# Gathers of the next expert moved, in pairs, to the first products of the present one, in a pooled-attention and mixture-of-experts kernel

## The chip, the cores and the metric

One NeuronCore of a Trainium2 chip runs the whole program. The metric is the device time of one execution in microseconds (us), inputs and output in HBM. TensorE (PE) multiplies, VectorE (DVE) and ScalarE (ACT) work on tiles in SBUF and PSUM, GpSimd (POOL) does some sums and issues the indirect transfers (gathers and scatters by a list of rows), and SyncE (SP) issues the plain transfers. Each engine takes its instructions strictly in order and waits for others by semaphores. SP's and POOL's transfers share 16 DMA engines.

## The reference

```python
# attention with keys and values pooled over 8 tokens, then:
logits = x @ w_gate
noisy = logits + log1p(exp(x @ w_noise)) * noise
top2 = the two best experts of each token; top2_w = softmax of their two values
out = 0
for e in range(8):
    for k in range(2):
        mask = top2[:, k] == e
        h = maximum(x[mask] @ w1[e], 0)              # 512 -> 1024
        out[mask] += top2_w[mask, k, None] * (h @ w2[e])   # 1024 -> 512
```

There are 4608 tokens of 512 numbers, so an expert sees about 1152 of them. Everything is float32.

## The kernel before

**Order of the work.** Attention comes first, then expert 0, then experts 1 to 7 one after another. Products are made of three TensorE passes on operands split into a high and a low part (ACT casts the high part, DVE subtracts to get the low part; function `parts`, lines 1336 and 1337).

**An expert is a list of 44 items.** `first_products(e)` makes items g0 to g0+21: the first layer of seven 128-token tiles, done with seven block products in place of eight (their sums are made by `sums_a` on POOL, from the quarters of w1, and by `sums_b` on DVE, from the quarters of the turned rows). The products come in the order A12·B21 (g0, g0+1), A11·B11 (g0+2, g0+3), four tail products (g0+4 to g0+7, the first layer of tiles 7 to 9), S1·T1 (g0+8, g0+9), S2·T2, S4·B22, S3·T3, four tail products, A22·T4 (g0+20, g0+21). From m0 = g0+22 on come the second-layer items: two for each of seven tiles (`second_tile`, m0 to m0+13), then eight of the second tail (`second_tail`, line 1502, m0+14 to m0+21). In expert 7 the second tail comes ahead of the tiles. A tail's width is chosen at run time from the expert's count of rows: 240 columns in experts 1, 6 and 7, 280 in 3 and 5, 304 in 2 and 4.

**Operand buffers.** Every item reads one or two of eight buffers `OPS`. `build(i)` fills, in order of use, every buffer that item i has set free, as soon as `ripe` and `gate` allow. So DVE and ACT work up to eight operands ahead of TensorE. The main loop writes, for each item: its matmuls, then what `todo` holds for it (`on(i, f)`), then its `after` (results read out of PSUM), then `build(i)`.

**The next expert's rows.** Each tile of 128 rows takes a chain: a POOL gather from x_dram into one of two `row` buffers (line 771), four SP writes into one of four `via` buffers in HBM (776), one SP load into one of four `xg` buffers (779), and then DVE's block transpose (`turn_rows`, 1308; for tiles 7 to 9 `tail_rows`, lines 818 to 823, with an ACT cast and a DVE subtraction). Before the change tiles 0 to 3 are gathered at g0+15 and g0+18, tiles 4 to 9 one by one at m0+1 to m0+8, each in the same place in which an earlier tile is turned; tails are turned at m0+10 to m0+12.

**Second-layer results.** `prev` (line 1124) gathers with POOL what a token's first visit left in slot_dram, into one of three `pv` buffers; `finish` adds the new result on DVE (1140) and lets POOL write it to slot_dram (1144) and scatter it to the output (1148). Before, `prev` for tile n+3 stands behind `finish` of tile n, and takes the same buffer.

**What sets the order.** PE, DVE, ACT and POOL run this part in the order in which the code stands (`manual_schedule`). SP's order is a scheduler's, with `turn_of` chaining some transfers. SP also loads w1 (`load_w1`, 1298) and halves of w2 (`wload`, 470), which ACT and DVE split at lines 490 and 491, one step every other item from g0+1 to g0+15.

Of the kernel before, what the change touches and what calls it, by code (L numbers as in the profile page):

```python
# [19 lines left out]
def kernel(  # L20
# [12 lines left out]
    nc = tc.nc  # L33
# [4 lines left out]
    P = 128  # L38
# [709 lines left out]
    XG = {}  # L748
    turns = {}

    def turn_of(q, make):
        if q in turns:
            with tc.issue_after(turns[q].ins):
                turns[q] = make()
        else:
            turns[q] = make()
        return turns[q]
# [25 lines left out]
    NM = 7  # L783
# [555 lines left out]
    def side_a(e, name, k):  # L1339
        def make(t):  # L1340
            src = sx(k) if name in ("S1", "S2") else {"A11": W1R[:, 0, k], "A12": W1R[:, 0, 2 + k], "A21": W1R[:, 1, k], "A22": W1R[:, 1, 2 + k],
                   "S3": W1R[:, 0, k], "S4": W1R[:, 0, 2 + k]}[name]
            parts(src, DF // 2, t)
            if name == "A11":
                sums_a(k, 1)
            elif name == "S1":
                sums_a(k, 2)
        return make

    def side_b(e, name, k):  # L1350
        def make(t):
            src = {"B11": XR1[:, 0, k], "B21": XR1[:, 0, 2 + k], "B22": XR1[:, 1, 2 + k], "T1": XR1[:, 0, k],
                   "T2": XR1[:, 0, k], "T3": XR1[:, 1, k], "T4": XR1[:, 0, 2 + k]}[name]
            parts(src, HN, t)
            if name == "B11":
                sums_b(k, 1)
            elif name == "T1":
                sums_b(k, 2)
        return make

# [108 lines left out]
    def second_tile(e, tt, n):  # L1469
        for j in range(2):  # L1470
            key = (e, "h", tt, j)
            makers[key] = side_h(tt, j)

            def run(j=j, key=key):
                if j == 0:
                    st[e, "y"] = bank()
                py = st[e, "y"]
                for f in range(4):
                    for i, (a, b) in enumerate(PASSES):
                        mm(py, at[key][:, a * DF // 2 + f * P:a * DF // 2 + (f + 1) * P], w2s(e, b, 4 * j + f),  # L1480
                           j == 0 and f == 0 and i == 0, j == 1 and f == 3 and i == 2)

            def after():
                finish(e, tt, P, st[e, "y"], st[e, "pv"].pop(0))
                if n + 3 < NM:
                    st[e, "pv"].append(prev(e, TILES[n + 3], P))
            item([key], run, after if j else None)

    def second_tail(e):
# [40 lines left out]
    def on(i, f):  # L1530
        todo.setdefault(i, []).append(f)

    def flush():
        with tc.issue_after(sent[-1].ins):
            nc.gpsimd.drain()

    gate, ripe = {}, {}
    for e in range(1, E):
# [21 lines left out]
        for i in range(8):  # L1560
            on(g0 + 1 + 2 * i, lambda: wadvance(1))
        for i in range(4 if e == 1 else 3):
            on(g0 + 8 + 2 * i, lambda: pend.pop(0)())
        if final:
            for i in range(3):
                on(m0 + 5 + 2 * i, lambda: pend.pop(0)())
# [2 lines left out]
            st[e, "pv"] = [prev(e, TILES[n], P) for n in range(3)]  # L1569
        on(m0 - 2, start_pv)  # L1570
        if e == 1:
            def visits2():
                with tc.issue_after(st["dve"].ins):
                    second_visits()

            def over2():
                with tc.issue_after(st["dve"].ins):
                    st["over"] = over_table()
            on(g0 + 9, visits2)
            on(g0 + 16, over2)  # L1580
        if not final:
            n = e + 1
            on(g0 + 15, lambda n=n: gathers(n, 0, 1))
            on(g0 + 18, lambda n=n: gathers(n, 2, 3))
            for i, j in ((0, 1), (0, 0), (1, 0), (1, 1)):
                on(m0, lambda n=n, i=i, j=j: load_w1(n, i, j))
            plan_ = ((1, 0, 4), (2, 1, 5), (4, 2, 6), (5, 3, 7), (7, 4, 8), (8, 5, 9), (9, 6, None))
            for d, a, b in plan_:
                on(m0 + d, lambda n=n, a=a: turn_rows(n, a))
                if b is not None:  # L1590
                    on(m0 + d, lambda n=n, b=b: gathers(n, b))
            for i in range(3):
                on(m0 + 10 + i, lambda n=n: tail_rows(n))
            on(m0 + 13, lambda: (sums_a(0, 0), sums_a(1, 0)))
            gate[n] = m0 + 13

    for i, g in enumerate(groups):
        if joined(g):
# [12 lines left out]
            gathers(1, 4, 5, 6)  # L1611
        elif i == 0:
            stage2(g, lambda t, mm: hook(i, t, mm), None)
    for i in range(3):
        on(i, lambda: tail_rows(1))
    on(2, lambda: (sums_a(0, 0), sums_a(1, 0)))
    gate[1] = -1
    ripe[1, "S1"] = 2

    def ready(key, i):  # L1620
        e = key[0]
# [25 lines left out]
            makers[key](OPS[s])  # L1647

    ET = mybir.EngineType
    with tc.manual_schedule(engines={ET.PE, ET.DVE, ET.Activation, ET.Pool}):  # L1650
        for t in range(4, NM):
            turn_rows(1, t)
        gathers(1, 7, 8, 9)
        build(-1, ())
        stage2(groups[2], None, None)
        TB.append(mp.tile([P, NFB * DF], F32, tag="hb", name="tb"))
        for i, (keys, run, after) in enumerate(items):
            build(i - 1, keys)
            run()
            for f in todo.get(i, ()):  # L1660
                f()
            if after:
                after()
            build(i, ())
# [93 lines left out]
```

## Time and profile before

| | |
|---|---|
| median of 3 runs | 1062.95 us (1062.29 to 1071.74) |
| the profiled execution's own time | 1062.45 us |
| its span in the trace | 1060.6 us |
| busy share of the span: PE, DVE, ACT, POOL | 93%, 68%, 44%, 48% |
| mean granted TensorE clock | 0.962 of full |
| experts 1 to 7 on TensorE | from 292.36 us to 1049.94 us |

Times in the rows are microseconds from the span's start. "Idle before" is time in which that engine had nothing running, with the event that ended it. A wait for several semaphores is put down to the last of them.

### The profile page before, as it was taken

Reading aid. Unit: us, or ns where it says so; the run is one execution under the profiler, and the core shown is the slowest. Engines: PE = TensorE matmul, PEld = TensorE weight load, DVE = VectorE, ACT = ScalarE, POOL = GpSimd, SP = SyncE. Lnnn points to the kernel's source line nnn. Section 1 sums busy time; section 2 is a strip of 40 time slices with the busy share of each in tenths; the row PEclk is TensorE's granted clock in tenths of the full one; section 3 lists DMA queues with packets and bytes.
Section 4 is the critical chain, followed back from the end, with each engine's and each line's share of the span. In section 5 each row is a group of like instructions: output and inputs, shape, how many; then the busy total and the mean of one; then the engine's idle time right before and its main releaser. Section 6 shows DMA issues by size and latency. Waiting matters only on the chain. (4 is left out here: it accounts for less than half of the span.)

```text
span 1060.6 us, 17080 instructions
## 1 busy us (share of the span) xinstructions
PE 982.3 (93%) x5684; PEld 878.0 (83%) x5684; DVE 716.8 (68%) x1503; ACT 463.3 (44%) x1130; POOL 505.9 (48%) x547
## 2 busy tenths in 40 slices
PE   7999998999978986999799979997999899979995
PEld 6898887789968866998799879986998789869984
DVE  6798787823489636964697469645975597459751
ACT  5778687401235403641274127412651265126520
POOL 3026587583142345554455445544554556345434
PEclk9999999999999996999899989998999899979998
DMA  9996845426735653476347644675476547753243
GB/s 301 319 329 210 265 150 164 113 58 164 239 115 176 187 165 118 148 220 205 123 145 244 188 138 147 203 209 157 126 246 210 162 130 250 209 161 112 82 136 135
DMA packets 141836, 189.91 MB, mean 179 GB/s; under 512 B 28992, under 2 KB 84945, under 8 KB 141722
## 3 DMA queue, kind: packets, MB, share of 16 engines
q1 hardware_dynamic: 114138, 121.77, 37.8%
q0 software_dynamic: 25472, 66.56, 19.9%
q8 instruction: 71, 1.16, 0.5%
q14 instruction: 43, 0.35, 0.1%
q10 hardware_dynamic: 2112, 0.07, 0.1%
HBM read 125.84 MB, written 70.25 MB: 185 GB/s over the span
## 5 line engine op out<-in xcount | busy, mean ns | idle before, releaser
L1411 PE MATMUL bank<-w,op 128*128 128x512 f32 x1176 | 267.8, 389 | 0.0
L1411 PEld LDWEIGHTS bank<-w,op 128*128 128x128 f32 x1176 | 220.7, 188 | 45.6
L1411 PE MATMUL bank<-op,op 128*128 128x448 f32 x1176 | 248.0, 370 | 9.9 <-DVE op L1337 5.5
L1411 PEld LDWEIGHTS bank<-op,op 128*128 128x128 f32 x1176 | 221.6, 190 | 31.1 <-DVE op L1337 7.9
L1502 PE MATMUL bank<-op,w 128*128 128x240 f32 (+2 forms) x672 | 109.2, 327 | 43.4 <-ACT op L1336 28.2
L1502 PEld LDWEIGHTS bank<-op,w 128*128 128x128 f32 x672 | 103.1, 223 | 49.6 <-ACT op L1336 30.6
L1124 POOL DMA_INDIRECT pv<-slot_dram,der x70 | 74.9, 1070 | 128.1 <-DMA via<-row 49.7
L771 POOL DMA_INDIRECT row<-x_dram,raw x70 | 83.3, 1190 | 109.6 <-DMA via<-row 92.8
L1308 DVE STREAM_TRANSPOSE xr<-xg 128x512 f32<-128x512 f32 (+1 forms) x56 | 53.3, 964 | 96.7 <-DMA xg<-via 96.5
L1374 ACT ACTIVATE op<-tb 128x512 fp32r<-128x512 f32 (+1 forms) x112 | 61.3, 575 | 114.0 <-PE bank L1411 76.5
L652 POOL DMA_INDIRECT rec_dram<-rec,pos x72 | 78.4, 1089 | 52.6 <-DVE rec L649 20.7
L1375 DVE SCALAR_TENSOR_TENSOR op<-tb,op 128x512 fp32r<-128x512 f32 (+1 forms) x112 | 66.4, 619 | 40.7 <-ACT op L1374 33.3
L823 ACT CAST xh<-tb 128x512 fp32r<-128x512 f32 (+1 forms) x21 | 11.5, 549 | 182.7 <-DVE tb L818 182.7
L1426 PE MATMUL bank<-xh,op 128*128 128x240 f32 (+2 forms) x448 | 86.2, 288 | 0.4 <-issue 0.3
L1140 DVE SCALAR_TENSOR_TENSOR pv<-bank,raw,pv 128x128 f32<-128x128 f32 x196 | 54.7, 341 | 43.9 <-PE bank L1411 34.9
L1337 DVE TENSOR_TENSOR op<-xr,op 128x448 fp32r<-128x448 f32 x98 | 79.5, 816 | 0.0
L1426 PEld LDWEIGHTS bank<-xh,op 128*128 128x128 f32 x448 | 71.0, 189 | 1.3 <-ACT tb L1444 0.5
L394 ACT ACTIVATE ex<-s,mx 128x72 f32<-128x72 f32 x284 | 69.3, 345 | 5.2 <-DVE mx L392 5.0
L420 PE MATMUL a<-vbd,eT 112*128 112x162 f32 (+3 forms) x480 | 70.0, 292 | 0.0
L1336 ACT CAST op<-xr 128x448 fp32r<-128x448 f32 x98 | 55.1, 569 | 28.2 <-PE bank L1411 9.7
L1144 POOL DMA_DIRECT2D slot_dram<-pv x55 | 32.1, 584 | 70.3 <-DVE pv L1140 64.2
L1426 PE MATMUL bank<-xl,op 128*128 128x240 f32 (+2 forms) x224 | 64.3, 287 | 0.0
(213 smaller groups left out, 1658.4 us busy)
## 6 DMA issues: line engine op xcount, KB each, us to landing
wst<-in_moe_w_dram SPq DMA_DIRECT2D x36, 512.0 KB
via<-row SPq DMA_DIRECT2D x266, 64.0 KB
xg<-via SPq DMA_DIRECT2D x63, 256.0 KB
w1r<-in_moe_w_dram SPq DMA_DIRECT2D x28, 512.0 KB
slot_dram<-pv POOLq DMA_DIRECT2D x55, 256.0 KB
k<-in_k_dram SPq DMA_DIRECT2D x7, 1280.0 KB
v<-in_v_dram SPq DMA_DIRECT2D x16, 512.0 KB
x_dram<-xr SPq DMA_DIRECT2D x16, 512.0 KB
```

Source lines behind the costliest of these rows:

```text
L394: lasta[0] = nc.scalar.activation(ex[:, jj, EPOS[h] * G:(EPOS[h] + 1) * G], sv[:, i], AF.Exp, bias=mx[:, i:i + 1])
L420: nc.tensor.matmul(a[ts_, half, (hs[0] % 4) * VW:(hs[-1] % 4 + 1) * VW], eT[:BST, n, ts_], vb[:BST, SLOT0[n]:SLOT0[n] + len(hs), :], start ...
L652: s = spaced(lambda: nc.gpsimd.indirect_dma_start(out=rec_dram[:, :], out_offset=bass.IndirectOffsetOnAxis(ap=pos[:, i, c:c + 1], axis=0), ...
L771: turn_of("pool", lambda: nc.gpsimd.indirect_dma_start(out=row[:32 * nr], out_offset=None, in_=x_dram[:, :], in_offset=bass.IndirectOffset ...
L1124: turn_of("pool", lambda: nc.gpsimd.indirect_dma_start(out=pv[:np_], out_offset=None, in_=slot_dram[:P + e * CAP, :], in_offset=bass.Indir ...
L1336: nc.scalar.copy(hv, src)
L1337: nc.vector.tensor_sub(lv, src, hv.bitcast(F32))
L1374: nc.scalar.activation(hv[:, :, c0:c1], src, AF.Relu)
L1375: nc.vector.scalar_tensor_tensor(lv[:, :, c0:c1], src, 0.0, hv[:, :, c0:c1].bitcast(F32), op0=OP.max, op1=OP.subtract)
L1411: last_pe[0] = nc.tensor.matmul(o, l, r, start=start, stop=stop, skip_group_check=True)
L1426: nc.tensor.matmul(part(ph), at[ks[db]][:, a * DF // 2 + f % 4 * P:a * DF // 2 + (f % 4 + 1) * P], part(xs[b][:, db]), start=(i == 0), sto ...
L1502: nc.tensor.matmul(part(st[e, "yb"][mb]), w2s(e, b, f)[:, mb * P:(mb + 1) * P], part(at[key][:, a * DF // 2:a * DF // 2 + NT]), start=(f = ...
```

## The change

- Gathers for expert e+1: tiles 0 and 1 at g0+2, tile 2 at g0+6, tile 3 at g0+11, 4 and 5 at m0, 6 and 7 at m0+2, 8 and 9 at m0+5. Rows are turned two tiles at a time at m0, m0+1, m0+5, m0+8 and m0+11, ahead of the gathers that share their place. The four loads of w1 go from m0 to m0+1, +3, +6 and +8.
- `prev` for tile n+2 is issued ahead of `finish` of tile n, so the buffer that it takes is that of tile n-1.
- `sums_a` of stages 0 and 1 and `sums_b` of stage 1 stand at g0 (`sums_a` of expert 1 at g0+2), not inside `side_a` and `side_b` and at m0+13.
- The late results of the tail tiles are finished at g0+7, +8, +9 (not +8, +10, +12).
- SP joins the engines whose order is the code's; `turn_of` then adds nothing.

```diff
     def turn_of(q, make):
+        if fixed[0]:
+            return make()
...
             parts(src, DF // 2, t)
-            if name == "A11":
-                sums_a(k, 1)
-            elif name == "S1":
+            if name == "S1":
                 sums_a(k, 2)
...
             parts(src, HN, t)
-            if name == "B11":
-                sums_b(k, 1)
-            elif name == "T1":
+            if name == "T1":
                 sums_b(k, 2)
...
             def after():
+                if 0 < n < NM - 2:
+                    st[e, "pv"].append(prev(e, TILES[n + 2], P))
                 finish(e, tt, P, st[e, "y"], st[e, "pv"].pop(0))
-                if n + 3 < NM:
-                    st[e, "pv"].append(prev(e, TILES[n + 3], P))
...
         for i in range(4 if e == 1 else 3):
-            on(g0 + 8 + 2 * i, lambda: pend.pop(0)())
+            on(g0 + 7 + i, lambda: pend.pop(0)())
...
+        d = 2 if e == 1 else 0
+        on(g0, lambda: (sums_b(0, 1), sums_b(1, 1)))
+        on(g0 + d, lambda: (sums_a(0, 0), sums_a(1, 0), sums_a(0, 1), sums_a(1, 1)))
+        ripe[e, "T1"] = g0
+        ripe[e, "S1"] = g0 + d
         if not final:
             n = e + 1
-            on(g0 + 15, lambda n=n: gathers(n, 0, 1))
-            on(g0 + 18, lambda n=n: gathers(n, 2, 3))
-            for i, j in ((0, 1), (0, 0), (1, 0), (1, 1)):
-                on(m0, lambda n=n, i=i, j=j: load_w1(n, i, j))
-            plan_ = ((1, 0, 4), (2, 1, 5), (4, 2, 6), (5, 3, 7), (7, 4, 8), (8, 5, 9), (9, 6, None))
-            for d, a, b in plan_:
-                on(m0 + d, lambda n=n, a=a: turn_rows(n, a))
-                if b is not None:
-                    on(m0 + d, lambda n=n, b=b: gathers(n, b))
-            for i in range(3):
-                on(m0 + 10 + i, lambda n=n: tail_rows(n))
-            on(m0 + 13, lambda: (sums_a(0, 0), sums_a(1, 0)))
-            gate[n] = m0 + 13
+            on(g0 + 2, lambda n=n: gathers(n, 0, 1))
+            on(g0 + 6, lambda n=n: gathers(n, 2))
+            on(g0 + 11, lambda n=n: gathers(n, 3))
+            for d_, i, j in ((1, 0, 1), (3, 0, 0), (6, 1, 0), (8, 1, 1)):
+                on(m0 + d_, lambda n=n, i=i, j=j: load_w1(n, i, j))
+            plan_ = ((0, (0, 1), (4, 5)), (1, (2, 3), ()), (2, (), (6, 7)), (5, (4, 5), (8, 9)),
+                     (8, (6, 7), ()), (11, (8, 9), ()))
+            for d_, a, b in plan_:
+                def step(n=n, a=a, b=b):
+                    for t in a:
+                        turn_rows(n, t) if t < NM else tail_rows(n)
+                    if b:
+                        gathers(n, *b)
+                on(m0 + d_, step)
+            gate[n] = m0 + 12
...
-    for i in range(3):
+    for i in (0, 0, 1):
         on(i, lambda: tail_rows(1))
-    on(2, lambda: (sums_a(0, 0), sums_a(1, 0)))
     gate[1] = -1
-    ripe[1, "S1"] = 2
...
-    with tc.manual_schedule(engines={ET.PE, ET.DVE, ET.Activation, ET.Pool}):
+    with tc.manual_schedule(engines={ET.PE, ET.DVE, ET.Activation, ET.Pool, ET.SP}):
+        fixed[0] = True
```

Left out: three `issue_after` lines (in `flush`, `visits2`, `over2`) that go, since their engines' order is the code's there already.

## Rows read from the trace of the kernel before

**Rows 1.** TensorE's waits: line, releaser: us in total, times, longest us.

```profile
PE bank L1502 <- ACT op L1336: 28.2, 10, 4.5
PE bank L1502 <- DVE op L1337: 13.5, 11, 5.7
PE bank L1411 <- DVE op L1337: 5.5, 5, 3.4
```

**Rows 2.** Windows over seven second tails: us, busy by engine, clock, DMA share, GB/s.

```profile
388.37:418.90 30.53, 16.70 (x98) 15.21 (x97) 13.38 (x28) 6.51 (x14) 12.48 (x14) 0.66 0.46 133
505.27:527.22 21.95, 16.35 (x97) 15.85 (x96) 12.33 (x23) 6.62 (x14) 10.11 (x11) 0.84 0.36 112
611.83:632.94 21.11, 15.47 (x97) 14.84 (x96) 11.83 (x23) 6.61 (x14) 9.61 (x11) 0.84 0.39 123
718.62:742.34 23.72, 16.82 (x97) 15.83 (x96) 14.66 (x30) 6.61 (x14) 10.60 (x12) 0.86 0.48 152
827.36:847.92 20.56, 15.83 (x97) 14.82 (x96) 11.78 (x24) 6.62 (x14) 9.71 (x11) 0.83 0.51 150
932.09:954.82 22.73, 16.04 (x97) 14.90 (x96) 13.34 (x29) 6.51 (x14) 10.14 (x12) 0.72 0.49 153
1000.90:1011.67 10.77, 10.77 (x97) 10.76 (x96) 5.61 (x9) 5.85 (x11) 0.00 (x0) 1.00 0.04 13
```

**Rows 3.** TensorE's timeline, expert 2: start, us, engine, line, operation, names, shape, count.

```profile
467.18 38.26 PE L1411 MATMUL bank<-w,op 128*128 128x512 f32 x168
505.27 8.43 PE L1502 MATMUL bank<-op,w 128*128 128x304 f32 x60
```

**Rows 4.** Waits on tile xg from 430 to 550 us, then DVE's timeline there.

```profile
  DMA xg<-via: 19.1, 5
...
519.71 0.62 DVE L818 STREAM_TRANSPOSE tb<-xg 128x256 f32<-128x256 f32 x1
```

**Rows 5.** Waits of DVE, of POOL and of SP's queue, over the span.

```profile
DVE xr L1308 <- DMA xg<-via: 96.5, 27, 9.2
...
POOL pv L1124 <- DMA out_dram<-pv,der: 37.1, 13, 5.2
...
SPq L776 <- DMA row<-x_dram,raw: 151.4, 42, 12.6
```

**Rows 6.** POOL's timeline in the second tiles of expert 2.

```profile
501.32 0.58 POOL L1144 DMA_DIRECT2D slot_dram<-pv  x1
502.21 1.00 POOL L1148 DMA_INDIRECT out_dram<-pv,der  x1 [0.30 <-issue]
506.60 1.00 POOL L1124 DMA_INDIRECT pv<-slot_dram,der  x1 [3.39 <-DMA out_dram<-pv,der]
507.91 0.93 POOL L771 DMA_INDIRECT row<-x_dram,raw  x1 [0.30 <-issue]
```

**Rows 7.** SP's timeline in the same stretch; four writes, then a load.

```profile
506.12 1.93 SPq L776 DMA_DIRECT2D via<-row  x4
...
516.39 0.34 SPq L779 DMA_DIRECT2D xg<-via  x1
```

**Rows 8.** TensorE's timeline at the first products of expert 1.

```profile
300.81 6.47 PE L1411 MATMUL bank<-op,op 128*128 128x448 f32 x24 [3.42 <-DVE yt L1190]
...
320.62 18.78 PE L1411 MATMUL bank<-op,op 128*128 128x448 f32 x83 [3.40 <-DVE op L1337]
```

**Rows 9.** The end: DVE's last sums, POOL's last write (timelines).

```profile
1050.84 1.13 DVE L1140 SCALAR_TENSOR_TENSOR pv<-bank,raw,pv 128x128 f32<-128x128 f32 x4 [5.17 <-DMA pv<-slot_dram,der]
...
1053.76 0.56 POOL L1144 DMA_DIRECT2D slot_dram<-pv  x1
```

**Rows 10.** First products of expert 3: POOL's timeline, then TensorE's.

```profile
540.82 1.69 POOL L1321 TENSOR_TENSOR tb<-w1r 128x512 f32<-128x512 f32 x1 [1.82 <-DVE op L1337]
...
561.12 3.44 POOL L771 DMA_INDIRECT row<-x_dram,raw  x1 [0.30 <-issue]
...
543.28 19.62 PE L1411 MATMUL bank<-op,op 128*128 128x448 f32 x96
```

More of the change, by code (lines that the diff above doesn't have):

```diff
@@ L749 @@
     turns = {}
+    fixed = [False]
     def turn_of(q, make):
+        if fixed[0]:
+            return make()
         if q in turns:
@@ L1533, in flush @@
     def flush():
-        with tc.issue_after(sent[-1].ins):
-            nc.gpsimd.drain()
+        nc.gpsimd.drain()
     gate, ripe = {}, {}
@@ L1571 @@
         if e == 1:
-            def visits2():
-                with tc.issue_after(st["dve"].ins):
-                    second_visits()
             def over2():
-                with tc.issue_after(st["dve"].ins):
-                    st["over"] = over_table()
-            on(g0 + 9, visits2)
+                st["over"] = over_table()
+            on(g0 + 9, second_visits)
             on(g0 + 16, over2)
+        d = 2 if e == 1 else 0
[3 more added lines that the diff above has]
+        ripe[e, "S1"] = g0 + d
         if not final:
             n = e + 1
-            on(g0 + 15, lambda n=n: gathers(n, 0, 1))
-            on(g0 + 18, lambda n=n: gathers(n, 2, 3))
-            for i, j in ((0, 1), (0, 0), (1, 0), (1, 1)):
-                on(m0, lambda n=n, i=i, j=j: load_w1(n, i, j))
-            plan_ = ((1, 0, 4), (2, 1, 5), (4, 2, 6), (5, 3, 7), (7, 4, 8), (8, 5, 9), (9, 6, None))
-            for d, a, b in plan_:
-                on(m0 + d, lambda n=n, a=a: turn_rows(n, a))
-                if b is not None:
-                    on(m0 + d, lambda n=n, b=b: gathers(n, b))
-            for i in range(3):
-                on(m0 + 10 + i, lambda n=n: tail_rows(n))
-            on(m0 + 13, lambda: (sums_a(0, 0), sums_a(1, 0)))
-            gate[n] = m0 + 13
+            on(g0 + 2, lambda n=n: gathers(n, 0, 1))
[13 more added lines that the diff above has]
+            gate[n] = m0 + 12
     for i, g in enumerate(groups):
```

## The prediction

> **What bounds the kernel now.** I read TensorE's waits first, since it is busy for most of the span, then cut the places of those waits into windows, and then looked at what DVE, POOL and SP did in one of them. The waits are nearly all at one line, the second tail, 1502, and their releasers are the two halves of an operand, ACT's cast and DVE's subtraction [rows 1]. The windows show the same place in every expert: six tails take 20.6 to 30.5 us, while the seventh, that of expert 7, which has no next expert to fetch, takes 10.77 us without a gap and at a granted clock of 1.00 [rows 2]. The six have 0.66 to 0.86, a mean over idle time and stretches at the lower of the two levels. So a tail loses in two ways, and both go if its operands are there in time.
>
> Why they are late is seen on DVE. Its instructions stand in one queue, and the transposes of the next expert's rows stand among the operand subtractions. Around expert 2's second tiles DVE sat idle for 19.1 us in five waits for loads of xg [rows 4]; over the span the transposes of line 1308 alone waited 96.5 us [rows 5]. Behind each wait stand the subtractions for TensorE and the sums of `finish`, and behind those POOL's queue.
>
> The chain that feeds xg is long, not wide. Tile 9 of expert 3: gather at 507.91 [rows 6], load of xg at 516.39 [rows 7], transpose at 519.71 [rows 4]: 11.8 us from gather to use. POOL starts a new one late, because ahead of it stands `prev`, which takes the buffer that `finish` has just begun to write out: 502.21 + 1.00 ends the issue of that scatter, and `prev` starts 3.39 us later [rows 6]. That wait alone is 37.1 us over the span [rows 5].
>
> **The change part by part.**
>
> *The gathers go earlier, in pairs.* Tiles 0 to 3 are gathered 7 to 13 items earlier, so they lie in xg long before m0. A second-layer item takes 38.26 us / 14 = 2.73 us [rows 3]. Tiles 6 and 7 have the six items from m0+2 to m0+8, 16.4 us; 8 and 9 the six from m0+5 to m0+11, the same; 4 and 5 the five from m0, 13.7 us, but nothing holds POOL back there, so they start before TensorE reaches m0. A pair needs the 11.8 us of one chain, a second gather, 0.93 + 0.3 us [rows 6], and a second set of four writes, 1.93 us [rows 7]: 15.0 us. That fits in 16.4 us, less what POOL has ahead of it, one `finish` of 0.58 + 1.00 us and two gaps of 0.3 us [rows 6]. So a wait of 1 to 2 us per pair can stay on DVE. It costs nothing: DVE works up to eight operands ahead, and 19.1 us of waits [rows 4] cost expert 2 only the 8.7 us worked out below, so some 10.4 us are covered. If that cover were gone, three waits of 2 us would cost 6 us per expert.
>
> *What that gives.* The full width of 304 columns takes 8.43 us for 60 matmuls, of which the last one's end overlaps; start to start I take 0.1383 us, so 96 take 13.28 us [rows 3]. For 240 columns 10.77 us are measured [rows 2]; for 280 I interpolate 12.34 us. The six tails then lose 19.76, 8.67, 8.77, 10.44, 8.22 and 11.96 us [rows 2], **67.8 us** together, slow stretches included. I take all of it. Bounds: nothing at all, if the waits only move, and 67.8 us, since the tail can't be shorter than its matmuls.
>
> *`prev` one tile later.* It now takes the buffer whose scatter was issued a tile earlier, two items or 5.5 us before; the scatter needs 3.4 us [rows 6], so POOL doesn't wait. The result is wanted two tiles, 10.9 us, after the issue. POOL's work from m0 to m0+13 is 4 `prev` of 1.3 us, 7 `finish` of 2.2 us and 6 gathers of 1.24 us [rows 6], 28 us of 38.2 us. What is queued behind a `prev` that waits is `finish` of that tile and the next pair of gathers. At the very end this pays directly: DVE's last sum started at 1050.84 us, having waited for such a gather, TensorE's last matmul ended at 1049.94 us, and POOL came to the last write only at 1053.76 us, with two finishes queued ahead [rows 9]. With the queue empty the sum ends near 1051.1 us and the write follows: **2.6 us**; bounds 0 and 2.6.
>
> *The sums at g0.* Their number is the same. DVE's four leave the place between the operands for g0+2 and g0+3, POOL's two for A11 no longer wait in turn. The price would be that S1·T1 at g0+8 has to wait for them; TensorE is short of an operand there already, 5.5 us over the span, of which 3.4 us in expert 1 [rows 1, 8]. In steady experts DVE reaches g0 without arrears, so the 2.1 us of small waits should go. In expert 1 the results of expert 0's tail are read out ahead of the sums, which removes most of the 3.42 us at 300.81, but its tail rows now stand ahead of S1 and two gathers stand ahead of the second sums. Of the 8.9 us I take **3.5 us**; bounds 0 and 8.9 (a loss here is the rival below).
>
> *SP in the code's order.* No transfer is added. SP waits for a row, and behind it stand loads of w1 and halves of w2. The last quarter of w1 leaves behind the loads of tiles 8 and 9, near m0+8, and is first wanted by POOL's sums at g0, 14 items later. Halves of w2 are issued eight items before they are split. I take 0; the other end is a rival. *The late finishes* at g0+7 to g0+9 are the same instructions up to three items earlier; they free the buffer that tile 3's load needs at g0+11. I take 0, and at most the few us by which POOL would be late there.
>
> *Sum.* 67.8 + 2.6 + 3.5 = 73.9 us, from the profiled execution's own 1062.45 us: **989 us**. It is 0.5 us under the median, so the same holds against the median. With all of the bounds at their best 983 us, with the last two terms at nothing and 1 us of new waits per expert 1001 us.
>
> **The rivals.**
>
> *Gathers stretched beside a busy DVE.* A gather takes POOL 0.93 us [rows 6], but one at 561.12, while DVE added results, took 3.44 us [rows 10]. The change puts two in that company, ahead of the second stage-2 sum, which ended its first half at 540.82 + 1.69 = 542.5 us [rows 10]. Two such gathers with their gaps are 7.5 us: 550.0 us, and S2·T2's second half begins after 36 of the 96 matmuls from 543.28, at 550.6 us [rows 10]. Cast and subtraction still have to follow, so TensorE waits some 1 us; in expert 1, where both sums stand behind the gathers, some 4 us. With 6 + 4 us back: **998 us**. Against it: DVE comes to S1 earlier than before. The Trainium skill (SBUF — State Buffer, section "SBUF: two separate sides") says more than this row: DVE in some modes shuts GpSimd out of a shared port, and GpSimd then can't write the descriptors of its own transfers; it would put every early gather at risk. The trace has both kinds, 3.44 and 0.93 us, so by that rule the time is this rival's.
>
> *The chain stays half late.* With two row buffers a second pair can't be gathered before the first is written out. If that leaves 15 us of DVE waits per expert, 4.6 us over the cover, six experts lose 28 us: **1016 us**. For it: SP waited 151.4 us for rows [rows 5]. Against it: POOL's queue no longer has the 3.4 us waits in it.
>
> *No gain.* The waits only move to the xg loads at m0+5 to m0+11, at the same length: about 1060 us. The chain of 11.8 us against 16.4 us speaks against it.
>
> *SP blocks, slower than before.* SP in the code's order waits for the rows of a gather while a half of w2 stands behind it; ACT and DVE then stop at the splitting and TensorE after them. From the issue at g0+5 to the use at g0+13 there are eight items of at most 19.62 / 8 = 2.45 us [rows 10], 19.6 us. Every us by which SP is later than that is lost in each of six experts, and from 19.6 + 73.9 / 6 = 32 us on the kernel is slower than before; at 35 us it would take 6 × 15.4 = 92 us, so **1081 us**. Waits for a row were 3.6 us in the mean (151.4 us in 42) and 12.6 us at the longest [rows 5]; three of the longest in one expert would do it.
>
> **How the numbers follow.** Forecast 0.68; stretched gathers 0.13; half late 0.10; no gain 0.04; SP blocks 0.05. The range of 981 to 1010 us holds the forecast with its bounds, 983 to 1001 and some 2 us of a run's scatter below, and the first rival: 0.8. The runs of before lie within 0.9% of each other, so about 1% is what a measurement can tell from no change. Faster by more than that: 0.68 + 0.13 + 0.10 = 0.91; within: 0.04; slower: 0.05.
>
> **What would show it.** Right: the second tails of experts 1 to 6 take 10.8 to 13.3 us at a granted clock near 1.00; TensorE's waits at line 1502 all but vanish; DVE's waits for xg fall from some 19 us per expert to under 6; POOL's `prev` no longer waits for a scatter; POOL's last write starts within 1.5 us of TensorE's end. Wrong: TensorE waits at line 1411 for S1 or S2 operands behind POOL's sums (first rival), DVE still waits over 10 us per expert for xg (second), or ACT waits at line 490 for wst (the last). What would upset the sum most is a new wait in expert 1, whose start is the least like the others.

## The result and the profile after

The changed kernel takes 1011.45 us (median of 4 runs, 1008.18 to 1017.61) and the kernel before, on the same chip, 1064.44 us (1062.29 to 1071.74): a ratio of 0.9497, 95% interval 0.9429 to 0.9566. It is 5% faster; 989 us was forecast, a ratio of 0.930. The profiled execution took 1017.61 us with a span of 1015.7 us, 6 us over the median. Against the median the forecast is 22.5 us short. The stages below are read in the profiled execution: 73.9 us off the span of 1060.6 us of before would have left 986.7 us, and it is 29.0 us longer than that.

The second tails first, as windows: us, busy time of PE, PEld, DVE, ACT and POOL, granted clock, DMA share, GB/s.

```profile
392.48:406.81 14.33, 11.72 (x97) 11.53 (x96) 7.32 (x19) 5.97 (x12) 5.83 (x7) 0.95 0.52 181
496.82:510.04 13.22, 13.22 (x97) 13.22 (x96) 6.79 (x16) 4.19 (x7) 9.49 (x9) 1.00 0.34 111
597.54:609.80 12.26, 12.26 (x97) 12.26 (x96) 5.91 (x13) 4.20 (x7) 9.35 (x10) 1.00 0.42 136
696.64:709.86 13.22, 13.22 (x97) 13.22 (x96) 7.04 (x17) 4.20 (x7) 8.78 (x9) 1.00 0.40 143
796.96:809.23 12.27, 12.27 (x97) 12.26 (x96) 6.63 (x16) 4.20 (x7) 9.14 (x9) 1.00 0.41 141
896.32:907.08 10.76, 10.76 (x97) 10.76 (x96) 5.46 (x15) 4.34 (x8) 6.55 (x7) 1.00 0.49 175
958.58:969.35 10.77, 10.77 (x98) 10.77 (x97) 5.61 (x9) 5.78 (x11) 0.00 (x0) 1.00 0.02 4
```

Against [rows 2], five of the six are gapless, at the full clock, and as long as forecast (13.28, 12.34 and 10.77 us by width). Only expert 1's keeps a gap.

The waits of TensorE, of DVE and of POOL over the span (line, releaser: us, times, longest):

```profile
PE bank L1411 <- DVE op L1341: 20.8, 14, 3.3
PE bank L1426 <- ACT tb L1444: 5.3, 2, 4.9
PE bank L1502 <- DVE op L1341: 2.6, 1, 2.6
...
DVE pv L1144 <- DMA pv<-slot_dram,der: 39.7, 13, 5.8
...
DVE tb L822 <- DMA xg<-via: 15.2, 9, 2.9
DVE xr L1312 <- DMA xg<-via: 15.0, 5, 11.3
...
POOL pv L1128 <- DMA out_dram<-pv,der: 49.4, 10, 7.2
```

TensorE's waits at line 1502 have gone from 41.7 us [rows 1] to 2.6, and DVE's wait for transposes from 96.5 [rows 5] to 15.0. But the products at line 1411 wait 20.8 us in place of 5.5 [rows 1], and POOL's `prev` still waits for scatters.

The 49.4 us can't be set against the 37.1 us of [rows 5]. Of the waits that stand directly behind a scatter the profile puts only a part down to that scatter; in the kernel before it puts another 49.7 us down to a landing of via, as here in expert 2:

```profile
475.14 1.02 POOL L1148 DMA_INDIRECT out_dram<-pv,der  x1 [0.30 <-issue]
482.23 1.01 POOL L1124 DMA_INDIRECT pv<-slot_dram,der  x1 [6.07 <-DMA via<-row]
```

All of POOL's idle time ahead of `prev`, whatever ended it, is 128 us before and 98 us after, so it fell. What stays is uneven. Of the four `prev` that each of experts 1 to 6 issues between its second tiles, the first two wait 0.3 us after the change, the third 3.8 to 5.5 us and the fourth 6.5 to 7.2 us. Before, the fourth waited 3.4 to 5.2 us.

Read off TensorE's timeline, from the first matmul of one stage to that of the next, summed over the seven experts (us):

| | before | forecast | after |
|---|---|---|---|
| start of expert 1 | 292.36 | 292.4 | 294.25 |
| first products | 339.34 | 335.8 | 359.65 |
| second tiles | 266.87 | 266.9 | 266.88 |
| second tails | 151.37 | 83.6 | 86.83 |
| last matmul to the end of the span | 10.66 | 8.1 | 8.1 |

The tails gave back 64.5 us and the end 2.6; the first products, which should have gained 3.5, lost 20.3. These 23.8 us are most of the miss of 29.0 us. The start's 1.9 us lie ahead of the code that was moved.

One place shows the loss: the second tiles of expert 2 and the first products of expert 3 behind them, which begin at 510.04. First POOL's timeline, then DVE's, then TensorE's.

```profile
490.72 1.01 POOL L1152 DMA_INDIRECT out_dram<-pv,der  x1 [0.30 <-issue]
498.25 1.00 POOL L1128 DMA_INDIRECT pv<-slot_dram,der  x1 [6.52 <-DMA out_dram<-pv,der]
499.25 0.59 POOL L1148 DMA_DIRECT2D slot_dram<-pv  x1
...
503.81 0.57 POOL L1148 DMA_DIRECT2D slot_dram<-pv  x1 [0.78 <-DVE pv L1144]
...
511.85 2.55 POOL L1323 TENSOR_TENSOR tb<-w1r 128x512 f32<-128x512 f32 x2
514.36 2.53 POOL L1319 TENSOR_TENSOR w1r<-w1r 128x512 f32<-128x512 f32 x2
...
502.39 1.12 DVE L1144 SCALAR_TENSOR_TENSOR pv<-bank,raw,pv 128x128 f32<-128x128 f32 x4 [4.73 <-DMA pv<-slot_dram,der]
...
511.34 6.04 DVE L1341 TENSOR_TENSOR op<-xr,op 128x448 fp32r<-128x448 f32 x1
...
528.17 1.36 DVE L1341 TENSOR_TENSOR op<-xr,op 128x448 fp32r<-128x448 f32 x1
...
533.27 0.61 DVE L1341 TENSOR_TENSOR op<-xr,op 128x448 fp32r<-128x448 f32 x1
...
529.59 2.74 PE L1411 MATMUL bank<-op,op 128*128 128x448 f32 x12 [0.88 <-DVE op L1341]
533.94 14.66 PE L1411 MATMUL bank<-op,op 128*128 128x448 f32 x71 [1.61 <-DVE op L1341]
```

`prev` reaches its place directly behind the scatter whose buffer it takes and stands there for 6.52 us, where [rows 6] had 3.39. Behind it stand three `finish`, three `prev` of the tail, and then the sums that the change put at g0. DVE, too, stands for 4.73 us until what this `prev` fetches has landed. POOL begins the sums at 511.85, after the first product has begun. So it is in every expert: ahead of experts 2 to 7 POOL begins S1's sums 0.7 to 7.4 us behind the first product, where before the change it began them 4.2 to 5.6 us ahead of it. While the four sums run, a subtraction of DVE's takes 6.04 us, where others of its size take 0.6 us with POOL doing no sums. DVE's queue is 5.4 us late from there on, and the two operands that TensorE waits for, the second half of T1 and the first of T2, leave it at 529.53 and 533.88.

### The profile page after: what moved, and what is told of

Read it like the earlier page. It is cut to its first block, busy times and chain, and to the rows that moved or that the text cites. A ratio compares the mean times of both kernels' runs of the same rounds, so it can differ in the third digit from the quotient of the medians.

```text
span 1015.7 us, 17117 instructions
## 1 busy us (share of the span) xinstructions
PE 963.3 (95%) x5684; PEld 862.9 (85%) x5684; DVE 724.5 (71%) x1503; ACT 467.6 (46%) x1130; POOL 527.3 (52%) x547
## 3 DMA queue, kind: packets, MB, share of 16 engines
q0 software_dynamic: 25472, 66.56, 21.2%
## 4 chain that ended last, share of the span: by engine, by line
PE 46%; DVE 7%; DMA 4%; issue 3%; POOL 2%; SPq 0%; ACT 0%; POOLq 0%; DVEq 0%
PE bank L1411 35%; PE bank L1502 7%; DVE op L1341 4%; PE bank L1426 4%; DMA slot_dram<-pv 1%; DMA row<-x_dram,raw 1%; DVE tb L1448 1%; DVE w L491 1%; DVE xr L1335 1%; DVE yt L1511 1%; POOL tb L1325 0%; DMA via<-row 0%; DMA out_dram<-pv,der 0%; POOL out_dram L1152 0%; DMA pv<-slot_dram,der 0%
## 5 line engine op out<-in xcount | busy, mean ns | idle before, releaser
L1411 PE MATMUL bank<-op,op 128*128 128x448 f32 x1176 | 249.6, 370 | 20.8 <-DVE op L1341 20.8
L1128 POOL DMA_INDIRECT pv<-slot_dram,der x70 | 85.1, 1215 | 97.6 <-DMA out_dram<-pv,der 49.4
L775 POOL DMA_INDIRECT row<-x_dram,raw x70 | 74.1, 1058 | 90.2 <-DMA via<-row 74.1
L1375 DVE SCALAR_TENSOR_TENSOR op<-tb,op 128x512 fp32r<-128x512 f32 (+1 forms) x112 | 66.2, 618 | 45.2 <-ACT op L1374 33.8
L1426 PE MATMUL bank<-xh,op 128*128 128x240 f32 (+2 forms) x448 | 88.9, 294 | 5.6 <-ACT tb L1444 5.3
L1341 DVE TENSOR_TENSOR op<-xr,op 128x448 fp32r<-128x448 f32 x98 | 87.2, 895 | 1.9 <-ACT op L1340 1.9
L1502 PE MATMUL bank<-op,w 128*128 128x240 f32 (+2 forms) x672 | 85.4, 288 | 2.6 <-DVE op L1341 2.6
L1502 PEld LDWEIGHTS bank<-op,w 128*128 128x128 f32 x672 | 84.9, 190 | 3.3 <-DVE op L1341 2.8
L1426 PEld LDWEIGHTS bank<-xh,op 128*128 128x128 f32 x448 | 73.3, 195 | 6.7 <-ACT tb L1444 6.1
L1152 POOL DMA_INDIRECT out_dram<-pv,der x49 | 63.0, 1286 | 17.4 <-issue 11.8
L1340 ACT CAST op<-w1r 128x512 fp32r<-128x512 f32 x84 | 51.2, 626 | 44.4 <-PE bank L1502 23.7
```

What stands on the lines that cost most here:

```text
L775: turn_of("pool", lambda: nc.gpsimd.indirect_dma_start(out=row[:32 * nr], out_offset=None, in_=x_dram[:, :], in_offset=bass.IndirectOffset ...
L1128: turn_of("pool", lambda: nc.gpsimd.indirect_dma_start(out=pv[:np_], out_offset=None, in_=slot_dram[:P + e * CAP, :], in_offset=bass.Indir ...
L1152: s = turn_of("pool", lambda: nc.gpsimd.indirect_dma_start(out=out, out_offset=bass.IndirectOffsetOnAxis(ap=tokc[e, t][:np_], axis=0), in_ ...
L1340: nc.scalar.copy(hv, src)
L1341: nc.vector.tensor_sub(lv, src, hv.bitcast(F32))
L1375: nc.vector.scalar_tensor_tensor(lv[:, :, c0:c1], src, 0.0, hv[:, :, c0:c1].bitcast(F32), op0=OP.max, op1=OP.subtract)
```

## The experiments

All were timed against the kernel before on the same chip. Attention, ahead of expert 1, takes some 12 us more on some chips than on others (expert 1 starts between 281.5 and 296.7 us), so kernels are compared by their ratios and by the two stages that move. "Sum" is first products plus second tails. The stages and waits of a row are those of one profiled execution. Two of the changed kernel (after, after_again) differ by 1.8 us in the first products and by 2.1 us in the tails, so a difference of some 2 us between two rows tells nothing. "`prev` waits for scatters" is the profile's count, a part of the waits as said above. The last column has the shortest and the longest idle time ahead of the fourth `prev` of experts 1 to 6, whatever ended it.

| kernel | us, median | ratio, 95% interval | first products | tails | sum | `prev` waits for scatters | fourth `prev` |
|---|---|---|---|---|---|---|---|
| before | 1064.44 | 1 | 339.3 | 151.4 | 490.7 | 37.1 | 3.4–5.2 |
| after | 1011.45 | 0.9497 (0.9429–0.9566) | 359.7 | 86.8 | 446.5 | 49.4 | 6.5–7.2 |
| after_again | 1002.14 | 0.9521 (0.9476–0.9565) | 361.5 | 84.7 | 446.1 | 46.2 | 5.8–6.7 |
| sums_back | 992.06 | 0.9434 (0.9390–0.9479) | 344.9 | 88.7 | 433.6 | 39.8 | 5.8–6.3 |
| stage0_back | 995.27 | 0.9465 (0.9421–0.9509) | 350.8 | 85.1 | 436.0 | 46.1 | 5.7–7.1 |
| only_dve_sums | 993.67 | 0.9455 (0.9408–0.9503) | 345.1 | 87.1 | 432.2 | 39.6 | 5.6–6.5 |
| only_sums | 1060.15 | 1.0063 (1.0017–1.0108) | 351.7 | 145.4 | 497.1 | 36.4 | 3.4–4.1 |
| prev_back | 1020.84 | 0.9708 (0.9650–0.9766) | 372.4 | 88.5 | 460.8 | 117.4 | 5.5–7.3 |
| late_gathers | 1036.19 | 0.9856 (0.9809–0.9903) | 365.3 | 111.6 | 476.8 | 45.2 | 5.8–7.3 |
| sp_scheduled | 992.36 | 0.9435 (0.9387–0.9482) | 349.6 | 83.3 | 432.9 | 26.1 | 2.9–4.0 |
| w1_at_m0 | 985.72 | 0.9355 (0.9326–0.9385) | 342.0 | 83.3 | 425.3 | 27.0 | 2.2–3.8 |
| w1_again | 1012.21 | 0.9507 (0.9453–0.9561) | 353.8 | 83.3 | 437.1 | 42.1 | 5.4–7.6 |
| w1_last_pair | 1008.17 | 0.9505 (0.9449–0.9561) | 352.8 | 83.3 | 436.1 | 42.3 | 5.7–6.7 |
| w1_first_pair | 1001.36 | 0.9440 (0.9398–0.9482) | 345.4 | 83.3 | 428.7 | 20.9 | 2.5–3.3 |
| dve_sums_w1 | 979.95 | 0.9288 (0.9261–0.9316) | 337.3 | 83.3 | 420.6 | 24.0 | 2.4–3.4 |
| dve_sums_sched | 983.57 | 0.9324 (0.9299–0.9350) | 341.3 | 83.3 | 424.6 | 24.9 | 2.4–3.1 |

The last column splits the kernels in two. With the last two loads of w1 where the change has them it is 5.4 to 7.6 us; with them anywhere else, or with SP scheduled, 2.2 to 5.2 us.

The theories: **Q**, the sums stand in POOL's queue behind work that is late; **L**, the sums hold up DVE wherever they overlap it; **G**, the early gathers slow the first products; and, from the third batch on, **D**, the loads of w1 among the second tiles make the last scatters land late.

### Are the sums' new places the cost?

*sums_back*: in the changed kernel, all sums where they were before.

```diff
-        on(g0, lambda: (sums_b(0, 1), sums_b(1, 1)))
-        on(g0 + d, lambda: (sums_a(0, 0), sums_a(1, 0), sums_a(0, 1), sums_a(1, 1)))
+            on(m0 + 13, lambda: (sums_a(0, 0), sums_a(1, 0)))
+    # stage 1 back inside side_a (A11) and side_b (B11)
```

> The changed kernel with the operand sums at their former places, all else changed. Theory Q (place in the queue): at g0 POOL's sums stand behind the last two finishes and the three gathers for the tail, so they come late and S1 and T1 with them; undoing that brings the first products of experts 2 to 7 from a mean of 49.9 us back to 47, and the time to 990 to 998 us. Theory L (the lock): POOL's sums hold up DVE by the same few us wherever they stand; then the time stays at 1008 to 1014 us. Theory G (gathers): the early gathers are what makes POOL late in the first products; then it stays at 1006 to 1014 us too, and S1 still waits.

Measured: the first products fall by 16.6 us against after_again, by 14.8 against after. The sums' places are a large part of the loss.

*stage0_back*: only POOL's two stage-0 sums go back to m0+13.

```diff
-        on(g0 + d, lambda: (sums_a(0, 0), sums_a(1, 0), sums_a(0, 1), sums_a(1, 1)))
+        on(g0 + d, lambda: (sums_a(0, 1), sums_a(1, 1)))
+            on(m0 + 13, lambda: (sums_a(0, 0), sums_a(1, 0)))
```

> The changed kernel with only POOL's two sums for S1 (stage 0) back at m0+13, ahead of the tail's gathers; the two for A11 and DVE's four stay at g0. Theory Q: most of the loss goes, since S1's cast no longer waits for POOL: 995 to 1003 us. Theories L and G: 1008 to 1014 us.

Measured: 10.6 us of the 16.6. POOL does the same sums, only earlier in its queue. It speaks for Q; L alone doesn't explain it.

*only_dve_sums*: POOL's sums go back, DVE's stay at g0.

```diff
-        on(g0 + d, lambda: (sums_a(0, 0), sums_a(1, 0), sums_a(0, 1), sums_a(1, 1)))
+            on(m0 + 13, lambda: (sums_a(0, 0), sums_a(1, 0)))
+    # sums_a stage 1 back inside side_a (A11)
```

> The changed kernel with POOL's sums at their former places and only DVE's four at g0. Theory Q (POOL's place in its queue is what costs): as good as with all sums put back, 0.940 to 0.944 of the kernel before, some 3 us better than that if DVE's move also takes away the wait for expert 0's tail in expert 1 (forecast: 3.4 us). If DVE's sums at g0 cost as much as POOL's, it lies half way, near 0.947.

Measured: 345.1 us of first products, as with all sums back. DVE's sums at g0 cost nothing; 16.4 of the 16.6 us are POOL's. How much of that is POOL's lateness, and how much DVE's stop beside four sums in a row at the moment when its operands are wanted, these runs don't separate.

*only_sums*: the kernel before, with the sums at their new places and nothing else of the change. As I read the code, in expert 1 the third tail tile is then turned after the first sums and overwrites half of the first of S1's two sums, whose memory it shares, so one of the seven products of that expert is computed from other numbers. The instructions are the same.

```diff
+        on(g0, lambda: (sums_b(0, 1), sums_b(1, 1)))
+        on(g0 + d, lambda: (sums_a(0, 0), sums_a(1, 0), sums_a(0, 1), sums_a(1, 1)))
-            on(m0 + 13, lambda: (sums_a(0, 0), sums_a(1, 0)))
```

> The kernel before with the new places of the sums alone. Theory Q: POOL gets to the sums behind the tail's gathers there too, the first products of experts 2 to 7 grow by about 3 us each, and the time is 1075 to 1085 us. Theory L: DVE is held up no more than before, 1060 to 1068 us. If the sums at g0 help as forecast, 1058 to 1062 us.

Measured: first products 12.4 us longer, tails 6.0 us shorter. The time of 1060.15 us is under the 1075 to 1085 us that Q gave: the first products lost less than the 18 us it counted with, and the tails gave some back. Still, the sums at g0 cost in the kernel before too. So what they stand behind is not made by the change alone.

### What of the rest is needed?

*prev_back*: `prev(n+3)` behind `finish(n)` again.

```diff
-                if 0 < n < NM - 2:
-                    st[e, "pv"].append(prev(e, TILES[n + 2], P))
                 finish(e, tt, P, st[e, "y"], st[e, "pv"].pop(0))
+                if n + 3 < NM:
+                    st[e, "pv"].append(prev(e, TILES[n + 3], P))
```

> The changed kernel with the first-visit gather for tile n+3 behind the finish of tile n again. In POOL's queue this is nearly the same place; only the pair of row gathers between two tiles changes sides. If that order is what gives POOL its arrears at the end of the second tiles, the time falls to about 1005 us; if the wait for the scatter is the cause, which both orders have, it stays at 1008 to 1016 us, or grows by some us since the row gathers now stand behind the wait; the second tails stay free of gaps in either case.

Measured: the first products take 10.9 us more, and POOL's idle time ahead of `prev` rises from 93 to 135 us (the profile's count of 46.2 and 117.4 us overstates it, since it puts nearly all of these waits down to scatters here). The two orders take the same buffer; what differs is that with the new one a tile's row gathers lie between a scatter and the `prev` that waits for it.

*late_gathers*: tiles 0 to 3 are gathered at g0+15 and g0+18 again.

```diff
-            on(g0 + 2, lambda n=n: gathers(n, 0, 1))
-            on(g0 + 6, lambda n=n: gathers(n, 2))
-            on(g0 + 11, lambda n=n: gathers(n, 3))
+            on(g0 + 15, lambda n=n: gathers(n, 0, 1))
+            on(g0 + 18, lambda n=n: gathers(n, 2, 3))
```

> The changed kernel with the gathers of tiles 0 to 3 back at g0+15 and g0+18, the rest as changed. If early gathers are what the second tails gain from, DVE waits for xg again and the tails grow, by 10 us or more in sum. If it is the distance between gather and turn from m0 on (pairs, two to six items ahead), the tails stay within 3 us of the changed kernel's. Theory G (early gathers make POOL late in the first products): the first products fall by 10 us or more in sum; theory Q: by less than 4 us.

Measured: the first products don't get shorter (365.3 us), so G falls; the tails grow by 26.9 us, with DVE again in waits for rows:

```profile
DVE xr L1312 <- DMA xg<-via: 82.7, 33, 10.4
```

*after_again* is the changed kernel as it is, as a control on that chip.

> The changed kernel once more, as the measure for the others of this round, since attention takes some 10 us more or less from chip to chip. By every theory 0.950 of the kernel before, and first products of experts 1 to 7 of 356 to 362 us in sum.

Measured: the sum of the two stages repeats within 0.4 us of the first profile.

*sp_scheduled*: SP's order is the scheduler's again, with its chaining.

```diff
-    with tc.manual_schedule(engines={ET.PE, ET.DVE, ET.Activation, ET.Pool, ET.SP}):
-        fixed[0] = True
+    with tc.manual_schedule(engines={ET.PE, ET.DVE, ET.Activation, ET.Pool}):
```

> The changed kernel with SP's order left to the scheduler again and its transfers chained. If SP's order in the code is without a price and without a gain, the same within 3 us. If the scheduler puts loads of weights between the pairs, DVE waits some us more for xg, which the cover of 10 us per expert hides: the same within 5 us. A gain of the change that needs SP's order would show as second tails with gaps, 10 us or more in sum.

Measured: 13.3 us of the sum come back, and the fourth `prev` waits 2.9 to 4.0 us in place of 5.8 to 6.7. So SP's order has a price, and it is paid on POOL. SP's timeline told where to look. In the changed kernel, for expert 3's w1:

```profile
463.69 0.43 SPq L1302 DMA_DIRECT2D w1r<-in_moe_w_dram  x1
...
479.81 0.43 SPq L1302 DMA_DIRECT2D w1r<-in_moe_w_dram  x1
...
489.39 0.95 SPq L1302 DMA_DIRECT2D w1r<-in_moe_w_dram  x2
```

The last two, 1 MB, leave together at 489.39, behind tile 9's loads, and the scatter of 490.72 above is the one that took 6.52 us. In the scheduled order the last of the four leaves 6.5 us after the second tiles of expert 2 have begun (448.26 against 441.8), here 30.7 us after (489.39 against 458.7).

### Is it the loads of w1?

*w1_at_m0*: SP's order as in the change, the four loads at m0.

```diff
-            for d_, i, j in ((1, 0, 1), (3, 0, 0), (6, 1, 0), (8, 1, 1)):
+            for d_, i, j in ((0, 0, 1), (0, 0, 0), (0, 1, 0), (0, 1, 1)):
```

> SyncE in the code's order as in the change, only the four loads of the next expert's W1 back at the first second tile instead of the second, fourth, seventh and ninth. Theory D (those loads, moved into the second tiles, crowd the scatters of the results, which land late, so that GpSimd's waits on out_dram grow and everything behind them is late): the scatters land in about 3.5 us instead of 5.9 to 6.5, the waits pv<-out_dram on GpSimd fall from 46 us to about 26, the first products of the seven experts from 361.5 to about 350, the second tails stay at about 84; about 0.944 of the kernel before. Rival K (something else in the order that the scheduler gave SyncE): waits of 42 us and more, first products 358 to 364, about 0.952.

Measured: better than either expectation. The first products fall by 19.5 us, the tails to 83.3, the ratio to 0.9355. K falls: the code's order is even better than the scheduler's once the loads are early. The same place as above, now with the first products of expert 3 from 490.71 on (POOL, DVE, TensorE):

```profile
470.89 1.01 POOL L1152 DMA_INDIRECT out_dram<-pv,der  x1 [0.30 <-issue]
474.85 1.01 POOL L1128 DMA_INDIRECT pv<-slot_dram,der  x1 [2.94 <-DMA out_dram<-pv,der]
...
487.98 2.56 POOL L1323 TENSOR_TENSOR tb<-w1r 128x512 f32<-128x512 f32 x2
...
488.07 4.20 DVE L1341 TENSOR_TENSOR op<-xr,op 128x448 fp32r<-128x448 f32 x1 [0.86 <-ACT op L1340]
...
506.58 19.62 PE L1411 MATMUL bank<-op,op 128*128 128x448 f32 x96
```

The same scatter lands in 2.94 us, POOL's sums begin 2.73 us before the first product and no longer 1.81 us after it. DVE is held up there too (4.20 us), but ahead of time, and the 96 matmuls run without a gap.

The DMA engines' share (the number before the last) in the same ten microseconds, aligned by the first `finish`: in the changed kernel

```profile
485.00:495.00 10.00, 10.00 (x45) 8.26 (x44) 5.65 (x12) 2.79 (x8) 2.67 (x3) 1.00 0.74 211
```

and with the loads at m0

```profile
465.17:475.17 10.00, 10.00 (x46) 8.28 (x45) 5.53 (x12) 2.87 (x7) 2.91 (x4) 1.00 0.55 168
```

While POOL waits for this one scatter, from the end of its issue to `prev`, the share is 0.73 and 0.35. Another reading would be that the loads hold up what stands behind them in SP's own queue. They don't: DVE's waits for rows are as long with the loads at m0 as with them among the tiles, 32.5 against 30.2 us, and no sum on POOL waits for a landing of w1 in the trace of after. With the loads at m0:

```profile
DVE xr L1312 <- DMA xg<-via: 16.4, 7, 9.8
DVE tb L822 <- DMA xg<-via: 16.1, 11, 2.2
```

*w1_again*: the loads at m0, and the last two a second time, with the same data, at the places of the change.

```diff
-            for d_, i, j in ((0, 0, 1), (0, 0, 0), (0, 1, 0), (0, 1, 1)):
+            for d_, i, j in ((0, 0, 1), (0, 0, 0), (0, 1, 0), (0, 1, 1), (6, 1, 0), (8, 1, 1)):
```

> All four loads of W1 at the first second tile, and the last two of them a second time, with the same data, where the change has them (seventh and ninth second tile): everything is early, and only the transfers beside the last scatters are back. If the crowding of those scatters is the cause (theory D), GpSimd's waits pv<-out_dram go from 27 us back to 45 or more, the first products from 342 to 355 to 362 us, and the ratio to about 0.952. If what counts is that the loads were early (theory E: something waited for W1 itself), the first products stay at 340 to 345 us and the ratio at 0.936.

Measured: w1 is there early, and still 11.8 of the 19.5 us are lost again, with POOL's wait at 42.1 us. SP's two repeated loads, and POOL's scatter and `prev`:

```profile
487.42 0.94 SPq L1302 DMA_DIRECT2D w1r<-in_moe_w_dram  x2
...
488.75 1.01 POOL L1152 DMA_INDIRECT out_dram<-pv,der  x1 [0.30 <-issue]
495.57 1.00 POOL L1128 DMA_INDIRECT pv<-slot_dram,der  x1 [5.81 <-DMA out_dram<-pv,der]
```

No sum waits for these transfers in the trace. Their company alone makes the scatter late, and it does so in each of the six experts (5.4 to 7.6 us). The first products (353.8 us) and the profile's count (42.1 us) fall a little short of D's 355 to 362 and 45, so two more kernels split the loads.

*w1_last_pair* and *w1_first_pair*: only the last two, or only the first two, of the four stand where the change has them.

```diff
-            for d_, i, j in ((0, 0, 1), (0, 0, 0), (0, 1, 0), (0, 1, 1)):
+            for d_, i, j in ((0, 0, 1), (0, 0, 0), (6, 1, 0), (8, 1, 1)):    # w1_last_pair
+            for d_, i, j in ((1, 0, 1), (3, 0, 0), (0, 1, 0), (0, 1, 1)):    # w1_first_pair
```

> First two loads of W1 at the first second tile, the last two at the seventh and ninth as in the change. If the last pair costs only by its company (theory D alone), it is as with the repeated loads: first products 352 to 356 us, GpSimd's waits pv<-out_dram 40 to 45 us. If the whole 19.5 us are the last pair's (theory E beside D: it also arrives too late), 358 to 363 us.

> The last two loads at the first second tile, the first two at the second and fourth, as in the change. If the first pair has a share of the cost, first products of 347 to 352 us (7.7 us over the 342 with all four early) and more of the waits pv<-out_dram than 27 us; if the last pair has all of it, 340 to 344 us.

Measured: the last pair costs 10.8 us, about the same as when it is only repeated (11.8), so its own lateness (theory E) costs nothing. The first pair costs 3.4 us, less than expected. The fourth `prev` isn't late with it; the third waits 4.0 to 5.0 us in place of 3.0 to 4.0. Together the pairs cost 17.7 to 19.5; the 3.5 to 5.3 us beyond the two single prices appear only with both and stay open.

### Both causes at once

*dve_sums_w1* (loads at m0 and POOL's sums at their former places, DVE's at g0) and *dve_sums_sched* (the same sums, SP scheduled) are the edits above put together.

> The same loads at the first second tile, and GpSimd's sums at their former places; VectorE's stay at the beginning. If the two savings (16.4 us of first products by the sums' places, 11.9 by SyncE's order) are of different causes, they add: first products 333 us, tails 84 to 87, about 0.928 of the kernel before. If both come only from GpSimd being late at the beginning of the first products, moving its sums away already takes most of it: first products 341 to 345, about 0.94. My guess is 340 and 0.937.

> GpSimd's sums at their former places, VectorE's at the beginning, and SyncE's order left to the scheduler. By the same two theories 333 or 341 to 345 us of first products. Against the kernel with the loads alone moved it tells whether anything but the loads' place counts in SyncE's order: under theory D the two agree within 4 us; under K this one alone has the shorter first products.

Measured: 337.3 and 341.3 us, where full addition would have given 333. The two savings overlap for the most part, as two cures of one illness do: with the loads early, POOL's sums at g0 cost 4.7 us and not 16.4. They lie 4.0 us apart, at the edge of what D allowed, and the scheduled one is the longer, against K. dve_sums_w1 is the fastest kernel, 0.9288 of the kernel before and 2.2% under the changed one by their ratios. What is left on TensorE there:

```profile
PE bank L1428 <- ACT tb L1446: 5.5, 1, 5.5
PE bank L1413 <- DVE op L1341: 5.3, 5, 1.4
```

## Why the prediction was wrong

**The steps that failed** are two, and they share most of the loss. The first is *SP in the code's order*: "No transfer is added ... I take 0." It asked when the last quarter of w1 is needed, 14 items later, and that was right. It did not ask what the quarter travels beside. The four loads were moved from m0 in among the second tiles, two of them directly beside the last scatter that a `prev` waits for. With nothing but their place put back, first products and tails together fall from 446.5 (446.1 repeated) to 425.3 us: 21 of the 29 us of the miss.

The second is *The sums at g0*: −3.5 us, which is of the wrong sign wherever POOL's sums stood there. All the sums at g0 cost 12.4 us of first products in the kernel before; POOL's alone cost 16.4 us in the changed kernel and 4.7 us with the loads at m0. "In steady experts DVE reaches g0 without arrears" holds for DVE, whose sums there cost nothing. It said nothing of POOL, which comes to g0 with the arrears of the second tiles, and there has all four sums in a row that had stood in two places before. Only DVE's sums at g0, with the loads at m0, leave the first products 2.0 us shorter than before, of the 3.5 forecast, and that is no more than two profiles of one kernel differ by. Expert 1 got the new wait that was feared: 4.9 us for a copy out of PSUM that ACT reaches only behind the casts of the tail rows.

**`prev` one tile later: "so POOL doesn't wait"** failed with them. It holds for the first two of an expert's four `prev`, and not for the other two. The 5.5 us between scatter and `prev` were counted in TensorE's items, but POOL has only gathers in between and comes to `prev` as soon as they are issued; so it stands there for what is left of the scatter. A round on POOL, from one write to the next, is then 0.58 + 0.30 + 1.01 us of write and scatter, the wait, and 1.0 us of `prev`: 5.8 us at a wait of 2.94 us, a little over the 5.5 us between two results, and 9.4 us at 6.52 us, which makes every `finish` behind it late. The 37.1 us from which the term started were themselves too few: they are the part of the waits that the profile puts down to scatters. The move itself is right: undone it costs 10.9 us in the first products.

**The tails: −67.8 us**, measured −64.5, and −68.1 in all seven kernels in which the loads' places or SP's order were altered. The gap in expert 1's tail, 3.6 us (1.4 in the repeat), is gone wherever the loads' places or SP's order were altered, even where one pair stayed late; why was not followed. The size, from the matmuls' own time with the seventh tail as the measure [rows 2], was right. Of the mechanism a part is shown: late_gathers loses 26.9 of the 66.7 us that after_again gained on the tails of before, so these are the early gathers' of tiles 0 to 3. The other 39.8 us, which the prediction put down to the pairs and to the chain of 11.8 us, come with the rest of the change and were not taken apart.

**The end: −2.6 us**, measured −2.56: TensorE ends at 1007.60 and POOL's last write starts 1.47 us later.

```profile
1007.64 1.13 DVE L1144 SCALAR_TENSOR_TENSOR pv<-bank,raw,pv 128x128 f32<-128x128 f32 x4 [4.31 <-DMA pv<-slot_dram,der]
...
1009.07 0.57 POOL L1148 DMA_DIRECT2D slot_dram<-pv  x1 [0.82 <-DVEq L1673]
```

**The rivals.** *Stretched gathers* named the place, S1 and S2 operands at line 1411 behind POOL's sums, but not the mechanism: the two gathers ahead of the second sum in expert 3 took 1.19 and 0.96 us. POOL's issues are stretched at another place: the scatter of the last tail tile took 5.5 us in each of experts 2 to 6 in the changed kernel, 1.4 us before. That alone is not the loss, since with the loads at m0 scatters of the tails took up to 7.3 us. *Half late* and *no gain* fall, since DVE's waits for xg went from 96.5 us at the tiles [rows 5] to 15.0, and from 45.2 us at the tail tiles to 15.2. *SP blocks* falls: ACT has no wait for wst in the trace of after. None of them held that a transfer off the path would make another one slow. The late finishes were not tried by themselves.

The terms add up: 27.1 us of the 29.0 lie in first products and tails (446.5 against the forecast 419.4). The loads' place and POOL's sums at g0 together account for 25.9 (446.5 to 420.6), and 1.2 are left; the other 1.9 are the start. How the 25.9 are shared depends on what is put back first: the loads alone give 21.2 and the sums then 4.7; the sums alone give 14.3 (only_dve_sums, 432.2) and the loads then 11.6.

## What to carry to other kernels

A transfer that nobody waits for can still set the time, through a short transfer beside it for which a queue stands still: when a load is moved, look at what is in flight at its new place and who waits for that, not only at its deadline. An engine's queue is late by everything in front; before work is moved to a stage's beginning, read on that engine's timeline when it gets there. And when a gain is lost elsewhere, two edits that each recover much of it, but not their sum, are a sign that both act through one place, here POOL's queue at the beginning of the first products; neither's price can then be given without saying where the other stands. Last, a wait that a profile puts down to one releaser is not all of that kind: add up the idle time ahead of the instruction before two kernels are compared by it.

## What the runs showed of the hardware

POOL stood for 2.9 us, from the end of its issue, for the scatter of a 128-row tile with the 16 DMA engines 55% busy in the ten microseconds around it, and for 6.5 us for the same scatter at 74%. The Trainium skill (DMA: Bandwidth & Descriptors, section "Latency and other measured facts") has the access latency of HBM rise from 0.2 to 2 us at high load; the trace agrees in kind. What it measures is the wait for a whole scatter and not one access, and that rose by 3.6 us.

A DVE subtraction with two operands in SBUF, otherwise 0.6 us, took 6.04 us where POOL did four sums on SBUF at the same time, and 4.20 us beside three; in the kernel before, 2.28 us beside two. The Trainium skill (SBUF — State Buffer, section "SBUF: two separate sides") has the two engines exclude each other in that case: whoever starts first keeps the shared ports for its whole instruction. The trace fits that in part. The subtraction ends 0.5 us after the last of POOL's four sums, which took 1.3 us each; but its record begins 0.51 us before the first of them, and it did not get its turn between two of them.
